# A GFNet filter with a ReGLU gate: the order of all steps written as a list, and the tenth pair of feature tiles multiplied in seven block products

## The chip, the cores and the metric

The kernel runs on one core of a Trainium2 chip. The time is that of the device for one execution, in microseconds (us). Several executions of the kernel before were timed; one more was taken by the hardware profiler, and all rows below are from that one.

The engines are TensorE (PE for matmuls, PEld for the loading of its weights), VectorE (DVE), ScalarE (ACT), GpSimd (POOL) and SyncE (SP), which here starts most DMAs. Each engine works through its own queue of instructions in the order of the program.

## The reference

```python
def _layernorm(x, axis=-1, eps=1e-5):
    m = jnp.mean(x, axis=axis, keepdims=True)
    v = jnp.var(x, axis=axis, keepdims=True)
    return (x - m) / jnp.sqrt(v + eps)
def _A_ref(x, w_r, w_i):                       # the filter
    X = jnp.fft.rfft2(x, axes=(-2, -1)) * (w_r + 1j * w_i)
    return jnp.fft.irfft2(X, s=x.shape[-2:], axes=(-2, -1))
def _B_ref(x, W_gate, W_up, W_down):           # ReGLU
    gate, up = x @ W_gate, x @ W_up
    return (gate * (gate > 0) * up) @ W_down
xn = _layernorm(x)                             # x: 1 x 2048 x 512, fp32
out = x + _A_ref(xn, w_r, w_i) * silu(_B_ref(xn, W_gate, W_up, W_down))
```

W_gate and W_up are 512 x 1376, W_down is 1376 x 512, the filter's weights are 2048 x 257. All is fp32.

## The kernel before

**Precision.** PE multiplies in fp16. Each operand is split into a high part, made by ACT or DVE, and a low part, the rest, made by DVE or POOL (the "lows"). A product is three passes, high x high, high x low and low x high (`PASSES`).

**The filter (branch A).** The two-dimensional transform is done by matmuls with constant matrices. Eight chunks of rows (`NCH`, c = 0 to 7) are loaded (x), normalised (xf), folded by symmetry (`fold`: eo, ee, xs), split (xs16) and multiplied by `first_stage`: a group of 24 matmuls on tiles of 64 (s in the profile), whose result t goes to memory (A_d) and comes back by frequency. Then eight middle chunks (`fft_chunk`) run through the stages y, xx, the multiplication with the weights wt on DVE and POOL (xsp, tt, pf), z and v. Last `last_stage` (again small tiles) and the unfolding by DVE give the filter's rows sv.

**The ReGLU (branch B).** Rows are taken in four blocks of 512 (c = 0 to 3), the 1376 features in eleven tiles of 128, the last one of 96. `turn` splits xf into x16 and transposes it by a DMA of SP's queue into xT, two chunks to a block, so block 1 needs chunks 2 and 3 (x16_2, x16_3). For each tile `product` makes gate and up (gu, 12 matmuls 128x512 each), `rectify` the ReLU of gate (r, on ACT), `hidden` the product h32 (DVE) and its split h16. `down` multiplies h16 with the split W_down (wds) into dn, one step of three matmuls for each tile and row group; `gate` takes silu (g). `down_weights` makes wds from the loaded W_down in place: the high of slot f (ACT) reads slot f + 1, and the low of slot f (DVE) reads it too, so that ACT's next slot waits for DVE's low. In the last block the last row group of dn is made in three pieces of columns: 256, 128 and 128 (`columns`).

**Fast pairs.** `PAIRS` joins ten of the tiles to five pairs. For a pair `fast_products` makes gate and up of both tiles in seven products of 12 matmuls 128x256 (sa, sb, sc), after the scheme of Strassen and Winograd, where the plain way takes four products of 12 matmuls 128x512. It needs the sums of rows xS (`row_sums`) and of weights wT (`weight_sums`), two copies on ACT (sb from sa, sk from sc) and two more adds on DVE (sc, se). Whether a pair is fast in block c is said by `fast(c, n)` from the table `FASTS`: with '2' from block 2 on, with '1' in block 3 alone. Before, pair 1, tiles 3 and 4, has '1', so nine pairs of blocks 2 and 3 are fast.

**The order.** Nothing runs while the kernel's functions are called. Each calls `step` (engine, cost, a function that issues the instructions, what it reads and writes), and `Plan` collects the steps. `Plan.run` then is a list scheduler: from a due time for each step (`DUES`), the leads of loads (`WAITS`), costs and the room of the buffers (`ROOM`) it picks the next step of an engine, with a bonus for PE to stay with tiles of one size. The steps are issued in the order that comes out. Buffers are taken in that order too, so which buffer a tile gets, and whom it waits for, follows from it.

A helper records every instruction, so nearly all rows of the profile have that one line (L200).

```python
def fast(c, n):
    return c >= NBL - int(FASTS[n])
```

Of the kernel before, what the change touches and what calls it, by code (L numbers as in the profile page):

```python
# [1572 lines left out]
```

## Time and profile before

| what | value |
|---|---|
| median of three runs | 400.47 us |
| the runs | 401.05, 399.61, 400.47 us |
| profiled execution: span | 399.6 us |
| PE busy | 391.2 us, 3332 matmuls |
| DVE, ACT, POOL busy | 329.2, 247.2, 72.3 us |
| moved by DMA | 69.55 MB, 174 GB/s on the mean |

The profiled execution lies at the lowest of the timed runs and 0.87 us below their median. In a row of the profile, `out<-in` are the program's names of what is written and read; `xN` is the number of instructions; what stands in brackets is the idle time ahead of a row and what ended it. The chain of waits goes back from the last instruction to what released each step.

Two coarser lines of the page show how the work lies over the span, in 40 slices of 10 us, each digit a busy share in tenths:

```profile
DVE  3899998998888997669986888988769863887995
ACT  6997986868576666845568865535335542754422
```

DVE is nearly full in the first 150 us and again at the end; ACT is fullest in the first 60 us.

### The profile page before, as it was taken

To read this page: it belongs to the slowest core of one execution; us is meant where nothing else is said; L and a number is where in the kernel's file an instruction comes from. 1 tells how busy PE (TensorE), PEld (TensorE's weight loads), DVE (VectorE), ACT (ScalarE), POOL (GpSimd) and SP (SyncE) were. 2 spreads that over 40 slices of the span, in tenths; PEclk is the share of its full clock that TensorE was granted. 3 is DMA by queue.
4 is the path that set the end of the run, shared out by engine and by line. 5 is a ranking of instruction groups with operands and counts; after the bars stand their busy time and mean duration, and the time that the engine had idled before them with its cause. 6 is when DMAs were issued, how large, how long until landed. Compare 5 with 4: busy or idle time off the path is not lost.

```text
span 399.6 us, 8608 instructions
## 1 busy us (share of the span) xinstructions
PE 391.2 (98%) x3332; PEld 243.8 (61%) x3332; DVE 329.2 (82%) x726; ACT 247.2 (62%) x479; POOL 72.3 (18%) x79
## 2 busy tenths in 40 slices
PE   6999999999999999999999999999999999999995
PEld 5965444544445444456585777776567878787544
DVE  3899998998888997669986888988769863887995
ACT  6997986868576666845568865535335542754422
POOL 1004300000000000051405391413212301122211
PEclk9899999999999999999999999999999999999999
DMA  7972311327812998997878790536543048998496
GB/s 272 407 230 63 106 54 34 100 55 178 294 55 51 307 307 244 279 268 167 215 222 246 223 241 22 146 81 199 153 125 107 2 106 183 228 296 167 133 239 158
DMA packets 59353, 69.55 MB, mean 174 GB/s; under 512 B 24688, under 2 KB 36560, under 8 KB 59312
## 3 DMA queue, kind: packets, MB, share of 16 engines
q1 hardware_dynamic: 57872, 66.38, 57.2%
q0 software_dynamic: 1440, 2.62, 4.3%
q8 instruction: 26, 0.43, 0.4%
q14 instruction: 15, 0.12, 0.1%
HBM read 43.81 MB, written 22.56 MB: 166 GB/s over the span
## 4 chain that ended last, share of the span: by engine, by line
PE 82%; DVE 8%; DMA 4%; ACT 3%; issue 2%; SPq 0%; DVEq 0%; ACTq 0%; POOLq 0%
PE dn L200 26%; PE gu L200 26%; PE sb L200 8%; PE sc L200 5%; PE sa L200 5%; PE z L200 3%; PE xx L200 3%; PE s L200 2%; DVE wgu L200 2%; PE y L200 2%; PE v L200 2%; DMA out<-sv 2%; DMA x<-in_x 2%; DVE sv L200 1%; ACT wgu L200 1%
## 5 line engine op out<-in xcount | busy, mean ns | idle before, releaser
L200 PEld LDWEIGHTS <-wgu 128*128 128x128 f16 x960 | 93.0, 98 | 65.3 <-issue 2.9
L200 PE MATMUL dn<-wds,h 128*128 128x512 f16 (+2 forms) x528 | 118.2, 373 | 0.3 <-DVE h L200 0.3
L200 PE MATMUL gu<-xT,wgu 128*128 128x512 f16 (+1 forms) x528 | 112.0, 369 | 0.4 <-DVE xT L200 0.4
L200 PEld LDWEIGHTS <-h 128*128 128x128 f16 (+1 forms) x594 | 53.5, 98 | 54.4 <-issue 2.8
L200 POOL TENSOR_TENSOR rp<-rp,rp 128x512 f32<-128x512 f32 x9 | 12.1, 1354 | 132.9 <-DVE pw L200 125.5
L200 PEld LDWEIGHTS <-wT 128*128 128x128 f16 x324 | 31.2, 98 | 6.1 <-issue 1.0
L200 PE MATMUL sb<-xS,wT 128*128 128x256 f16 x216 | 26.6, 273 | 0.0
L200 PE MATMUL sa<-xT,wgu 128*128 128x256 f16 x216 | 26.5, 273 | 0.0
L200 ACT ACTIVATE r<-gu 128x512 f32<-128x512 f32 (+2 forms) x26 | 14.9, 574 | 16.2 <-PE gu L200 16.2
L200 DVE TENSOR_TENSOR h<-gu,r 128x512 f32<-128x512 f32 (+3 forms) x34 | 20.6, 607 | 5.0 <-ACT h L200 3.5
L200 ACT ACTIVATE h<-h 128x512 f16<-128x512 f32 (+1 forms) x26 | 16.1, 624 | 11.8 <-DVE h L200 11.8
L200 DVE SCALAR_TENSOR_TENSOR tt<-xsp,cw,wt 128x512 f32<-128x512 f32 x32 | 22.8, 755 | 0.1
L200 ACT ACTIVATE g<-dn,cdi 128x512 f32<-128x512 f32 (+1 forms) x16 | 10.8, 673 | 16.5 <-PE dn L200 16.5
L200 DVE TENSOR_TENSOR h<-h,h 128x512 f16<-128x512 f32 (+1 forms) x26 | 18.3, 705 | 1.8 <-ACT h L200 1.7
L200 POOL TENSOR_TENSOR tt<-tt,tt 128x256 f32<-128x256 f32 x10 | 9.5, 957 | 43.1 <-DVE tt L200 41.1
L200 PE MATMUL gu<-xT,wgt 128*64 128x256 f16 (+1 forms) x144 | 17.0, 309 | 0.0
L200 ACT ACTIVATE a<-y 128x1024 f16<-128x1024 f32 x8 | 8.2, 1024 | 12.8 <-PE y L200 6.1
L200 DVE SCALAR_TENSOR_TENSOR wgu<-raw,p,wgu 128x512 f16<-128x512 f32 x20 | 15.1, 772 | 0.0
L200 POOL TENSOR_TENSOR pf<-tt,tt 128x256 f32<-128x256 f32 x12 | 11.3, 947 | 18.9 <-DVE tt L200 16.6
L200 DVE TENSOR_TENSOR a<-y,a 128x1024 f16<-128x1024 f32 x8 | 9.8, 1224 | 5.6 <-ACT a L200 5.5
L200 ACT ACTIVATE rp<-rp,csc 128x512 f32<-128x512 f32 x20 | 13.5, 713 | 1.1 <-DMA rp<-in_wg 1.1
L200 PEld LDWEIGHTS <-wgt 128*64 128x64 f16 (+1 forms) x144 | 9.6, 106 | 6.6 <-issue 1.3
(208 smaller groups left out, 701.2 us busy)
## 6 DMA issues: line engine op xcount, KB each, us to landing
A_d<-t SPq DMA_DIRECT2D x16, 256.0 KB, 3.8
rw<-in_wl SPq DMA_DIRECT2D x8, 512.0 KB, 5.2
wt<-in_wl SPq DMA_DIRECT2D x8, 512.0 KB, 5.5
at<-A_d SPq DMA_DIRECT2D x8, 512.0 KB, 5.1
C_d<-t SPq DMA_DIRECT2D x16, 256.0 KB, 3.5
ct<-C_d SPq DMA_DIRECT2D x16, 256.0 KB, 6.8
x<-in_x SPq DMA_DIRECT2D x7, 512.0 KB, 5.7
G_d<-g SPq DMA_DIRECT2D x12, 256.0 KB, 3.6
```

Of the source, the lines that this page charges most:

```text
L200: return lambda *args, **kw: self.tc.keep_in_program_order(f(*args, **kw))
```

## The change

The scheduler goes, and with it its two tables of numbers, `DUES` and `WAITS`. In their place stands one list, `ORDER`, of 1678 numbers: the steps are issued in this order. In `FASTS` the second entry goes from '1' to '2', so that pair 1 is fast in block 2 as well, and ten pairs are fast. Its sums of weights are thus made ahead of block 2 and no longer ahead of block 3. The number of steps goes from 1671 to 1678: on PE 424 to 427, DVE 553 to 555, ACT 411 to 413; POOL (73) and SP (210) keep theirs.

```diff
-FASTS = ['2', '1', '2', '2', '2']
+FASTS = ['2', '2', '2', '2', '2']
-DUES = (
-    78.44, 124.64, 138.03, 130.55, 999999976, 999999994, 999999984, 999999989, 999999991, 999999984, 999999981, 999999975, 999999987, 999999960,
...
-WAITS = (
-    34.96, 5.86, 10.55, 96.13, 0.66, 8.25, 139.72, 229.23, 74.47, 110.72, 71.7, 201.18, 86.45, 49.12, 48.58, 203.18, 90.2, 18.44, 50.66, 82.96, 4.33,
...
+ORDER = (
+    4, 5, 46, 6, 7, 8, 9, 10, 11, 12, 47, 71, 13, 70, 14, 15, 16, 17, 18, 19, 20, 21, 22, 23, 24, 25, 26, 228, 27, 28, 29, 30, 
...
     def run(self):
-        steps = self.steps
-        for s in reversed(steps):
...
-        for t, s in order:
-            s.fn()
+        for n in ORDER:
+            self.steps[n].fn()
```

The order moves over the whole program: a step stands on the mean 9 places (PE), 13 (DVE), 11 (ACT) or 13 (SP) from where it stood on its engine, some up to 170. Over the whole order PE's visits to groups of small tiles (s, y, z, v and the like, several groups in one visit) go from 31 to 25. The first product of block 1, gu1_0_0, stands right behind the last products of block 0 and one group of s (s1_2); before, all dn of block 0, the groups s1_0 and s1_1 and the product gu1_0_1 stood ahead of it, and 24 matmuls of dn and s1_0 were among the last products of block 0. The last dn of all is the piece of 128 columns, before it was that of 256. At the head of the program PE transposes the first rows (head) ahead of the `small` that sums m0, which it did behind it before, and ACT copies that head to xTf with no row of x2 in front, where xf2 stood in front of it.

Three places show what the rows look like (after a name the number of its buffer's use; L200 is the helper's line before, L154 after). First, DVE at about 60 us of the span: the splits of the rows x16_2, the folding eo1 of chunk 1 and the weights wds. Before:

```order
L200 TENSOR_REDUCE max_md_127<-rows_md_802 128x1
L200 TENSOR_TENSOR h32_0_5_822<-gu0_5_1_690,r0_5_704 128x512
L200 SCALAR_TENSOR_TENSOR wgu6_100<-raw6_1_655,p6_766,wgu6_100 128x512
L200 TENSOR_TENSOR xs16_2_820<-xs2_630,xs16_2_820 128x2x512
L200 TENSOR_TENSOR h32_0_7_841<-gu0_7_1_806,r0_7_789 128x512
L200 TENSOR_TENSOR xs0_711<-eo0_688 128x2x128
L200 TENSOR_SCALAR scd_114<-rho_108,pd_128 128x11
L200 TENSOR_TENSOR h16_0_5_825<-h32_0_5_822,h16_0_5_825 128x512
L200 SCALAR_TENSOR_TENSOR wds_107<-wds_107,scd_114 128x512
```

And now:

```order
L154 TENSOR_TENSOR x16_2_812<-xf2_461,x16_2_812 128x512
L154 TENSOR_REDUCE max_md_127<-rows_md_863 128x1
L154 TENSOR_TENSOR xs0_896<-eo0_835 128x2x128
L154 TENSOR_SCALAR scd_114<-rho_108,pd_128 128x11
L154 TENSOR_TENSOR xs16_2_882<-xs2_791,xs16_2_882 128x2x512
L154 TENSOR_TENSOR eo1_937<-xf1_309 128x2x257
L154 SCALAR_TENSOR_TENSOR wds_107<-wds_107,scd_114 128x512
L154 TENSOR_TENSOR h32_0_7_943<-gu0_7_1_839,r0_7_855 128x512
L154 TENSOR_TENSOR ee0_948<-eo0_835 128x2x129
L154 SCALAR_TENSOR_TENSOR wds_107<-wds_107,scd_114 128x512
```

The lows of x16_2 have moved up ahead of this place, and eo1, which takes the buffer of x16_2, stands between them and the first low of wds. The first of these rows is the second half of x16_2.

SP's queue at the same place holds the transposing DMAs of block 1's rows (xT1). Before they stand behind the stores of t:

```order
L200 DMA x4_796<-in_x 128x1024
L200 DMA x5_905<-in_x 128x1024
L200 DMA A_d_69<-t1_2_898 128x1x1024 x2
L200 DMA out_0<-in_x 128x512
L200 DMA A_d_69<-t1_0_960 128x1x1024 x2
L200 DMA_TRANSPOSE xT1_1122<-x16_2_1016 128x16x128
L200 DMA_TRANSPOSE xT1_1122<-x16_3_1059 128x16x128
```

Now:

```order
L154 DMA x5_724<-in_x 128x1024
L154 DMA_TRANSPOSE xT1_796<-x16_3_750 128x16x128
L154 DMA x4_800<-in_x 128x1024
L154 DMA_TRANSPOSE xT1_796<-x16_2_812 128x16x128
L154 DMA s4_130<-in_sp 128x16
L154 DMA out_0<-in_x 128x512 x2
L154 DMA A_d_69<-t1_2_968 128x1x1024 x2
```

Both transposes have moved up, that of x16_3 ahead of that of x16_2, and the loads of x4 and x5 stand between and before them.

Second, ACT somewhat later, where r0_8 reads the product gu0_8_0, whose buffer gu1_0_0 takes. Before:

```order
L200 ACTIVATE r0_7_789<-gu0_7_0_748 128x512
L200 ACTIVATE wgt_106<-raw6_0_383,p6_766 128x4x96
L200 ACTIVATE wgu6_100<-raw6_0_383,p6_766 128x512
L200 ACTIVATE r0_8_804<-gu0_8_0_776 128x512
L200 ACTIVATE xs16_2_820<-xs2_630 128x2x512
L200 ACTIVATE h16_0_5_825<-h32_0_5_822 128x512
```

Now:

```order
L154 ACTIVATE wds_107<-wds_107,scd_114 128x512 x2
L154 ACTIVATE t1_2_968<-s1_2_909 128x2x448
L154 ACTIVATE h16_0_6_971<-h32_0_6_793 128x512
L154 ACTIVATE wds_107<-wds_107,scd_114 128x512
L154 ACTIVATE t1_2_968<-s1_2_909 128x2x64
L154 ACTIVATE xf4_991,st4_992<-x4_800 128x512
L154 ACTIVATE r0_8_996<-gu0_8_0_865 128x512
```

r0_8 has moved from ahead of the first wds to behind four of them.

Third, DVE in block 2, at the last pair (2,9) of it, whose add sc2_4 stood and stands behind work of the middle chunks (xsp, tt). Before:

```order
L200 TENSOR_TENSOR sr2_3_3221<-sb2_3_3119,sr2_3_3221 128x512
L200 TENSOR_TENSOR p16_3_3399<-pf_3_3358,p16_3_3399 128x1024
L200 TENSOR_TENSOR xsp_4_3415<-xx4_3385,xo4_3418 128x256
L200 SCALAR_TENSOR_TENSOR tt3_4_3454<-xsp_4_3415,cw_110,wt_4_3027 128x512
L200 SCALAR_TENSOR_TENSOR tt2_4_3456<-xsp_4_3415,cw_110,wt_4_3027 128x512
L200 SCALAR_TENSOR_TENSOR tt1_4_3472<-xsp_4_3415,cw_110,wt_4_3027 128x512
L200 TENSOR_TENSOR sc2_4_3420<-sb2_4_3433,sk2_4_3452 128x512
```

Now:

```order
L154 TENSOR_TENSOR sr2_3_3632<-sb2_3_3409,sr2_3_3632 128x512
L154 TENSOR_TENSOR t9_4_3648<-v4_3611,t9_4_3648 128x2x512
L154 TENSOR_TENSOR h16_2_2_1_3577<-se2_2_3307,h16_2_2_1_3577 128x512
L154 TENSOR_TENSOR h16_2_3_0_3653<-sr2_3_3632,h16_2_3_0_3653 128x512
L154 TENSOR_TENSOR xsp_5_3712<-xx5_3655,xo5_3672 128x256
L154 SCALAR_TENSOR_TENSOR tt2_5_3724<-xsp_5_3712,cw_110,wt_5_3359 128x512
L154 SCALAR_TENSOR_TENSOR tt1_5_3726<-xsp_5_3712,cw_110,wt_5_3359 128x512
L154 SCALAR_TENSOR_TENSOR tt3_5_3728<-xsp_5_3712,cw_110,wt_5_3359 128x512
L154 TENSOR_TENSOR sc2_4_3675<-sb2_4_3670,sk2_4_3718 128x512
```

The middle chunk beside the pair is the fifth and no longer the fourth, and between sr2_3 and the add a store's split t9_4 and two h16 have come in where p16_3 stood.

More of the change, by code (lines that the diff above doesn't have):

```diff
@@ L62 @@
 TICK, TICK_TO = 1.16, 60
-FASTS = ['2', '1', '2', '2', '2']
+FASTS = ['2', '2', '2', '2', '2']
 XDUE, SDUE = [-44.18, 1.62, 81.91, 105.7, 173.95, 99.44, 177.4, 146.02], [-114.62, 32.24, 147.09, 211.35]
 DEVIATE = (2.68, 2.54, 2.54)
-DUES = (
-    78.44, 124.64, 138.03, 130.55, 999999976, 999999994, 999999984, 999999989, 999999991, 999999984, 999999981, 999999975, 999999987, 999999960,
-    999999983, 999999975, 999999990, 999999987, 1.00000001e+09, 999999988, 999999984, 999999986, 1e+09, 999999973, 999999995, 999999991, 999999991,
-    999999989, 999999986, 999999992, 999999993, 999999994, 1.00000001e+09, 999999994, 999999964, 999999992, 999999995, 999999996, 999999996,
-    999999999, 999999999, 999999984, 999999993, 1.00000002e+09, 999999998, 999999999, -215.98, -223.3, -206.7, -40.58, -39.53, -42.57, -38.17,
[87 rows of a table removed]
-)
-WAITS = (
[13 rows of a table removed]
+ORDER = (
[62 rows of a table added]
 )
@@ L255, in run @@
     def run(self):
-        steps = self.steps
-        for s in reversed(steps):
-            s.due = 1e9 if s.due is None else s.due
-            for d in s.deps:
-                t = s.due - d.cost - d.lag
-                d.due = t if d.due is None else min(d.due, t)
-        for s, due in zip(steps, DUES):
-            s.due = due
-        for s, lead in zip([s for s in steps if s.lead is not None], WAITS):
-            s.lead = lead
-        for s in steps:
-            if s.due > CALM and s.engine == "SP":
-                s.lag += SAFE_LAG
-            elif s.due > CALM and s.engine != "PE":
-                s.cost *= SAFE
@@ L271, in run @@
-        base = lambda n: n[0] if isinstance(n, tuple) else n
-        users, holds = {}, {}
-        for s in steps:
-            holds[s] = {base(n) for n in [*s.names, s.holder] if base(n) in self.tiles}
-            for n in holds[s]:
-                users[n] = users.get(n, 0) + 1
-        room = {t: [0.] * n for t, n in self.room.items()}
-        live, last = set(), {}
-        free = dict.fromkeys(("PE", "DVE", "ACT", "POOL", "SP"), 0.)
-        ports = {"DVE": 0., "POOL": 0.}
-        dma, todo, order, mode, port = 0., {e: [] for e in free}, [], 0, None
@@ L282, in run @@
-        waiting = {s: len(s.deps) for s in steps}
-        after = {}
-        for s in steps:
-            for d in s.deps:
-                after.setdefault(d, []).append(s)
-            if not s.deps:
-                todo[s.engine].append(s)
-        for _ in steps:
-            best = None
-            for e, mine in todo.items():
-                at = []
-                for s in mine:
-                    t = max([free[e]] + [d.end + (0. if d.engine == e == "PE" else d.lag + s.margin) for d in s.deps])
-                    if s.lead is not None:
-                        t = max(t, s.due - s.lead)
-                    if s.port:
-                        t = max(t, ports["POOL" if e == "DVE" else "DVE"])
-                    need = {}
-                    for n in holds[s] - live:
-                        tag = self.tiles[n][0]
-                        need[tag] = need.get(tag, 0) + 1
-                    if any(len(room[tag]) < k for tag, k in need.items()):
-                        continue
-                    for tag, k in need.items():
-                        t = max(t, sorted(room[tag])[k - 1] + .15)
-                    at.append((t, s))
-                if at:
-                    soon = min(t for t, _ in at) + .06
-                    now = [k for k in at if k[0] <= soon]
-                    if e == "PE" and mode:
-                        now = [k for k in now if 0 < k[1].mode < 3 and k[1].due < k[0] + JOIN] or now
-                    t, s = min(now, key=lambda k: (e == "PE" and k[1].mode != mode if mode else 0, k[1].due, k[1].order))
-                    late = [k for k in at if soon < k[0] <= t + .5 * s.cost and k[1].due < min(s.due, k[0]) + HURRY]
-                    if late and e in ("ACT", "DVE"):
-                        t, s = min(late, key=lambda k: (k[1].due, k[1].order))
-                    turns = best and s.port and best[1].port and {e, best[1].engine} == {"DVE", "POOL"} and abs(t - best[0]) < .03
-                    if best is None or (e != port if turns else t < best[0]):
-                        best = t, s
-            assert best, "no step can begin"
-            t, s = best
-            e = s.engine
-            todo[e].remove(s)
-            for n in holds[s]:
-                if n not in live:
-                    live.add(n)
-                    r = room[self.tiles[n][0]]
-                    r.remove(min(r))
-            if e == "PE":
-                t, mode = t if s.mode == mode else max(t, free[e] + MODE), s.mode
-            free[e] = t + s.cost
-            s.end = free[e]
-            if s.kb:
-                if s.block:
-                    s.end = free[e] = max(s.end, dma + s.block)
-                dma = max(dma, s.end) + s.kb / (340 if t < CALM else RATE)
-                s.end = dma
-            if s.port:
-                ports[e], port = s.end, e
-            for n in holds[s]:
-                users[n] -= 1
-                last[n] = max(last.get(n, 0.), s.end + s.lag)
-                if not users[n]:
-                    room[self.tiles[n][0]].append(last[n])
-            order.append((t, s))
-            for a in after.get(s, ()):
-                waiting[a] -= 1
-                if not waiting[a]:
-                    todo[a.engine].append(a)
@@ L351, in run @@
-        order.sort(key=lambda k: k[0])
-        self.log = order
-        for t, s in order:
-            s.fn()
+        for n in ORDER:
+            self.steps[n].fn()
 def dve(n):
```

161 rows, old and new, of tables (DUES, ORDER, WAITS) are left out of this document.

## The prediction

> **What bounds the kernel now.** I read the page first, then PE's waits, then the chain of waits in order of time, then windows of the start, and last the timelines of DVE and ACT where the change puts something new.
>
> ```profile
> PE 391.2 (98%) x3332; PEld 243.8 (61%) x3332; DVE 329.2 (82%) x726; ACT 247.2 (62%) x479; POOL 72.3 (18%) x79
> PEclk9899999999999999999999999999999999999999
> PE 82%; DVE 8%; DMA 4%; ACT 3%; issue 2%; SPq 0%; DVEq 0%; ACTq 0%; POOLq 0%
> ```
>
> PE is busy for 98% of the span at nearly full clock and holds 82% of the chain; the next engine, DVE, has 82% of the span to do. The waits of PE, all of them, are these (total, times, longest):
>
> ```profile
> PE gu L200 <- ACT xTf L200: 1.4, 1, 1.4
> PE small L200 <- DVE md L200: 1.1, 1, 1.1
> PE small L200 <- ACT wgu L200: 0.6, 1, 0.6
> PE gu L200 <- DVE xT L200: 0.4, 1, 0.4
> PE dn L200 <- DVE h L200: 0.3, 1, 0.3
> ```
>
> The first four lie ahead of 22 us; the last is at 377.8. Between them PE never waits. So the span is start + PE's work + tail, and a change can do four things: alter PE's work, alter the start, alter the tail, or make PE wait where it does not wait now. A written order in place of the scheduler's can do all four. One more thing belongs to the start:
>
> ```profile
> 0.00:60.00 60.00, 56.54 (x337) 36.28 (x338) 49.98 (x157) 50.74 (x126) 9.48 (x19) 0.97 0.55 188
> 7.14:10.55 3.41, 1.60 (x12) 1.32 (x13) 1.98 (x9) 2.32 (x8) 0.00 (x0) 1.00 1.02 401
> 10.55:13.96 3.41, 3.41 (x18) 3.41 (x18) 2.54 (x8) 3.41 (x9) 0.00 (x0) 0.50 1.04 412
> ```
>
> (Columns: length, busy PE, PEld, DVE, ACT, POOL, then the granted clock, DMA share, GB/s.) After a stretch in which PE was busy for 1.60 of 3.41 us, the clock was 0.50 for the next 3.41 us. That costs half of it, 1.7 us of PE's work.
>
> **The change part by part.** The sum is made against the profiled execution, span 399.6, which is 0.87 below the median of the runs, 400.47; I carry differences over to the median.
>
> *1. The start, up to block 1's first product.* To compare like with like I take the moment when PE has done all products of block 0 and one group of s, which is what the new order puts ahead of gu1_0_0. Before, by the chain (start, us):
>
> ```profile
> 67.51 1.94 PE dn L200 x9
> 69.46 0.78 PE s L200 x24
> 70.24 1.40 PE dn L200 x6
> ...
> 74.23 0.65 PE dn L200 x3
> ...
> 77.47 1.29 PE dn L200 x6
> 78.76 1.43 PE gu L200 x24
> ```
>
> The products of block 0 end at 78.76 + 1.43 = 80.19. The four pieces of dn (5.28) and this second group of s (0.78) go behind gu1_0_0 in the new order: 80.19 - 5.28 - 0.78 = 74.13. Two gains may bring PE there sooner. The first is at the head of the program:
>
> ```profile
> 7.80 0.64 PE L200 MATMUL head<-unit,xf 128*128 128x128 f32 x4
> ...
> 9.31 0.58 ACT L200 ACTIVATE xTf<-head 128x512 f32<-128x512 f32 x1
> ```
>
> The head ends at 8.44, but ACT copies it only from 9.31 on, since a load of x2 held xf2 ahead of the copy. In the new order nothing of x2 is ahead: 0.87. And head is no longer behind the `small` that waited 0.6 for wgu; half of that makes it 1.2. The second gain is the half clock (1.7), which a fuller window may spare. So PE arrives between 74.13 and about 71.2 (74.13 - 2.9); I take the middle, 72.6.
>
> PE may not start then, since gu1_0_0's buffer comes free only with ACT's r0_8. r0_8 stands in ACT's queue behind a ladder of wds pairs, where every ACT half waits for the DVE half before it, and the first DVE half stands behind eo1, which takes the buffer that the second transposing DMA reads (x16_2). That DMA comes from about 88 us down to about 60; ahead of it in SP's queue are now the other transpose and two loads of x. Its landing is the unknown:
>
> ```profile
> x<-in_x SPq DMA_DIRECT2D x7, 512.0 KB, 5.7
> x<-in_x SPq DMA_DIRECT2D x2, 256.0 KB, 2.6
> L200 SPq DMA_TRANSPOSE xT<-x x2: 1802/2210/2617, 87.9 to 90.6; - x2
> xS<-S_d SPq DMA_TRANSPOSE x4, 8.6
> ```
>
> The two transposes took 1.8 and 2.6 us on the queue; how long from issue to landing isn't shown. Bounds are 2.6 (a small load, also about the longer of the two queue times) and 8.6 (the other kind of transposing DMA); I take 5.7, the load with the same 512 KB. Then the ladder, by these rows of DVE and ACT:
>
> ```profile
> 61.50 0.69 DVE L200 TENSOR_TENSOR h<-gu,r 128x512 f32<-128x512 f32 x1
> 68.33 0.74 DVE L200 SCALAR_TENSOR_TENSOR wds<-wds,scd 128x512 f16<-128x512 f32 x1
> ...
> 69.11 0.72 ACT L200 ACTIVATE wds<-wds,scd 128x512 f16<-128x512 f32 x1 [0.96 <-DVE wds L200]
> 69.73 0.61 ACT L200 ACTIVATE h<-h 128x512 f16<-128x512 f32 x1
> 71.28 0.90 ACT L200 ACTIVATE t<-s 128x896 f16<-128x896 f32 x1
> ```
>
> Successive rows overlap by some 0.1, which I take off. From T0, the end of the second low of x16_2 on DVE: 5.7 to the landing; eo1 and a wds on DVE, 0.69 + 0.74 - 0.1 = 1.3; four more rows of DVE and the next wds, 1.8 (h 0.6, the rest short); then on ACT wds 0.65, t 0.83, h 0.53, wds 0.63, a short t 0.2, xf and r0_8 0.6 each, 4.0. Together 12.8. T0: by 60.00 DVE had begun 157 instructions, and the low is the 159th of the new order; two more at 60/157 = 0.38 us give 60.8, and I take 61.0. gu1_0_0 starts at 61.0 + 12.8 = 73.8, after a wait of 1.2, against 74.1: **-0.3**. Bounds: with a landing of 2.6 PE's own arrival decides, 71.2, so -2.9; with 8.6 it is 76.7, +2.6.
>
> *2. The tenth pair.* Pair (3,4) of block 2:
>
> ```profile
> 222.41 2.59 PE gu L200 x12
> 225.00 1.31 PE sb L200 x12
> ```
>
> Four plain products (gu) cost 4 x 2.59 = 10.36, seven fast ones (sb) 7 x 1.31 = 9.17: **-1.19**, all of it on PE, which waits for nothing there. The sums of weights are the same work, only earlier. Two copies on ACT and two adds on DVE come in (0.61 and 0.69 each); ACT, idle for 38% of the span, hides its part; DVE's part is in point 4. If the products had to wait for them all the gain would be gone, 2 x (0.61 + 0.69) = 2.6 against 1.19.
>
> *3. Fewer changes between small and large tiles.* The chain shows s groups (small tiles) alone and in one go:
>
> ```profile
> 341.07 0.78 PE s L200 x24
> 341.86 1.42 PE sc L200 x12
> ...
> 345.48 1.31 PE sa L200 x12
> 346.79 1.44 PE s L200 x48
> ```
>
> Two groups in one visit take 1.44, apart 1.56: 0.12 saved. The product behind a visit takes 1.42 instead of 1.31: 0.11 more. A visit saved is worth 0.23, or about 0.11 an edge. In the new order the visits fall from 31 to 25, one of them ahead of gu1_0_0; five at 0.23 give 1.15, less two edges that come in within visits: **-0.95**. The bounds are 0 (the edges hidden behind weight loads) and -1.4 (six whole visits).
>
> *4. New waits in block 2.* Ahead of the add sc2_4 on DVE now stand, from the product sr2_3 on, t9_4, two h16, three parts of xsp and three tt:
>
> ```profile
> 66.19 1.22 DVE L200 TENSOR_TENSOR xs<-xs,xs 128x1024 f16<-128x1024 f32 x1
> ...
> L200 DVE SCALAR_TENSOR_TENSOR tt<-xsp,cw,wt 128x512 f32<-128x512 f32 x32 | 22.8, 755 | 0.1
> ```
>
> t9_4 as the 1024-wide row, 1.22; h16 2 x 0.69; xsp 0.8 (512 columns in three parts); tt 3 x 0.755 = 2.27; the add 0.69; less 0.65 of overlaps: 5.7 us from the time when sr2_3 ends. PE has three fast products and two pieces of dn in that time, 3 x 1.31 + 2 x 0.65 = 5.2: a wait of 0.5. Behind PE's waiting product in its queue is everything else. Two other places of blocks 2 and 3 read alike with less in front, 0.3 each: together **+1.1**, bounds 0 (DVE is early there) and 2.1 (each twice as late).
>
> *5. The end.* The wait of 0.3 for h goes: **-0.3**. The last down piece becomes 128 columns wide, before it was 256:
>
> ```profile
> 395.01 0.47 ACT L200 ACTIVATE g<-dn,cdi 128x256 f32<-128x256 f32 x1 [2.92 <-PE dn L200]
> 395.51 0.42 DVE L200 TENSOR_TENSOR sv<-sv,g 128x256 f32<-128x256 f32 x1 [1.05 <-ACT g L200]
> ...
> 390.75 0.37 ACT L200 ACTIVATE g<-dn_3bb,cdi 128x128 f32<-128x128 f32 x1 [0.32 <-PE dn_3bb L200]
> ...
> 65.99 0.29 DVE L200 TENSOR_TENSOR t<-s,t 128x128 f16<-128x128 f32 x1 [0.97 <-ACT t L200]
> ```
>
> ACT 0.47 - 0.37 = 0.10, and DVE twice 0.42 - 0.29 = 0.13: **-0.36**, plainly behind PE's last matmul.
>
> Sum: -0.3 - 1.19 - 0.95 + 1.1 - 0.3 - 0.36 = -2.0. Span 399.6 - 2.0 = 397.6; time 400.47 - 2.0 = **398.5**.
>
> **The rivals.**
>
> *Slower: the transposing DMA is late.* It lands after 8.6, as xS does; for it speaks that two loads of 512 KB and another transpose are in the queue just ahead, against it that its queue times are no longer than 2.6. gu1_0_0 then starts at 76.7, 2.9 later than forecast: -2.0 + 2.9 = +0.9. PE has waited 76.7 - 72.6 = 4.1 by then, so some stretch of 3.41 has no more than the 1.60 of busy time that brought the half clock above, and 1.7 more are lost: 400.47 + 2.6 = **403.1**. It decides from a landing of about 7 on, where the wait passes 2 us. The Trainium skill, "TensorE: Matmul & The Clock Gate", Part 1: The HAM clock gate, says that the clock halves after an idle window of about 3.4 us that runs freely; by that rule a stretch with 1.60 of work is not idle, so the row above disagrees unless partial work counts, and this rival would end near 401.4 unless the wait covers such a window whole.
>
> *No change: DVE's queue.* DVE has only 18% of its time left and its order is now fixed. If the three waits of point 4 are twice as long (+1.1 more) and the edges of point 3 save half (+0.5), the sum is -0.4 and the time 400.47 - 0.4 = **400.1**. For it: three tt rows in a block ahead of an add; against: before had DVE rows of the same kind in front of the same add without a wait of PE. Here belongs also the case that the tenth fast pair gives nothing since its copies hold PE.
>
> *Better: the start gives more.* Landing by 4 us or less and no half clock: gu1_0_0 at about 72.2, another -1.6: 400.47 - 3.6 = **396.9**.
>
> **How the numbers follow.** Chances: forecast 0.45 (own range 397.6 to 399.8, from points 3 and 4); late DMA 0.15; no change 0.22; better 0.18. A measurement tells 0.3%, 1.2 us, from no change: bounds 399.27 and 401.67. Faster: 0.18 of the better case and 0.39 of the forecast's 0.45, 0.57. Slower: the late DMA and 0.01, 0.16. Same: 0.27. The range runs from 396.6 (a little under the better case) to 401.6 (no change with the worst waits, and the late DMA without the half clock); about 0.15 is left above and 0.05 below.
>
> **What would show it.** Point 1: gu1_0_0 near 73.8 with ACT r as its releaser, and a clock row of 1.00 at 10 to 14 us or again 0.50. Point 2: seven sa, sb, sc groups of 1.31 for pair (3,4) in block 2. Point 3: PE's work behind gu1_0_0 shorter by about 2.1. Point 4: three new rows in PE's waits with DVE sc or sb. Point 5: last matmul to end of span shorter by 0.36. A wait of PE of over 2 us anywhere, or a half clock past 22 us, would make the forecast wrong.

## The result and the profile after

| | before | after |
|---|---|---|
| median of six runs each, on one chip | 400.13 us | 402.80 us |
| lowest and highest | 399.20 to 401.05 us | 401.52 to 404.79 us |
| ratio after to before, 95% interval | | 1.0065 (1.0038 to 1.0092) |
| span of the profiled execution | 399.6 us | 401.7 us (its time 403.46) |

The change made the kernel 0.65% slower, 2.7 us; forecast were 2.0 us less. The time of a run is 1.8 us more than its span (403.46 to 401.7, and so in every run). The six runs after are of two kinds: with a mean granted clock of 0.999 they took 401.52, 401.71 and 402.14 us, with 0.992 to 0.994 403.46, 403.70 and 404.79. A stretch of 3.41 us at half clock takes 0.0042 off the mean; the profiled run, of the second kind, has one in the middle of the program. Against the 400.13 of before, the first kind is some 1.6 us slower (its median is 401.71) and the second some 3.6 (403.70). One execution of number 8 below took 506.68 us at a mean granted clock of 0.755 and is in none of the comparisons.

Busy time, the granted clock in 40 slices, and the chain by engine, from the page after:

```profile
PE 389.3 (97%) x3368; PEld 248.4 (62%) x3368; DVE 337.7 (84%) x728; ACT 244.9 (61%) x481; POOL 73.3 (18%) x79
PEclk9999999999999999999999999899999999999999
PE 46%; DVE 15%; DMA 2%; ACT 1%; issue 1%; ACTq 0%; DVEq 0%
```

PE has 1.9 us less to do, DVE 8.5 us more, of which the two new adds are 1.4. The shares of the chain add up to only 65%, since it is followed back no further than 135 us; in that part DVE holds 15%, where it held 8% of the whole chain before. The lower clock has moved from the second slice (10 us) to the 26th (250 us). PE's waits after, those of 0.7 us or more:

```profile
PE gu L154 <- DVE t L154: 2.2, 1, 2.2
PE sc L154 <- DVE sr L154: 2.0, 1, 2.0
PE small L154 <- ACT wgu L154: 1.1, 1, 1.1
PE small L154 <- DVE md L154: 1.1, 1, 1.1
PE gu L154 <- ACT r L154: 0.9, 2, 0.5
PE z L154 <- ACT xsp L154: 0.7, 1, 0.7
```

Three are new and lie in the middle of the program: 2.2, 2.0 and 0.7 us. Before, nothing behind 22 us waited longer than 0.3. Where they stand, with the first product of block 1 ahead of them, in PE's timeline (start, length; in brackets the idle time in front and who ended it):

```profile
72.53 2.75 PE L154 MATMUL gu<-xT,wgu 128*128 128x512 f16 x12 [0.47 <-ACT r L154]
...
148.32 4.20 PE L154 MATMUL gu<-xT,wgt 128*64 128x256 f16 x36 [2.20 <-DVE t L154]
...
200.46 1.50 PE L154 MATMUL z<-cD,p 128*128 128x128 f16 x24 [0.71 <-ACT xsp L154]
...
252.80 2.43 PE L154 MATMUL sc<-xS,wgu 128*128 128x256 f16 x12 [1.99 <-DVE sr L154]
```

gu1_0_0 starts at 72.53. The last row is one fast product, which takes 1.31 elsewhere; here it takes 2.43. Windows of the start, of the 3.41 us around that wait and of the 3.41 us that follow (columns as before):

```profile
10.24:13.65 3.41, 3.41 (x33) 3.41 (x33) 3.11 (x13) 3.41 (x10) 0.00 (x0) 1.00 1.04 419
249.72:253.13 3.41, 1.42 (x19) 0.68 (x17) 3.03 (x4) 0.89 (x1) 2.20 (x2) 1.00 0.00 0
253.13:256.54 3.41, 3.41 (x59) 2.50 (x56) 3.21 (x4) 2.80 (x6) 0.00 (x0) 0.50 0.00 0
```

The half clock at the start is gone; another one begins at 253.13, right behind the wait of 2.0. So each profile has one such stretch, and they cancel between the two. The difference of the spans, +2.1, adds up: up to gu1_0_0 -1.6 (72.53 against 74.13, with the half clock of before in it); the three new waits +4.9, the old one of 0.3 gone; the half clock at 253.13 +1.7 (half of 3.41); the tail behind PE's last matmul, 3.9 against 4.6, -0.7; and as the remainder PE's work behind gu1_0_0, -1.9. The same terms nearly give the medians. Most runs of before have no half clock (number 7), and against these the start is worth -1.6 + 1.7 = +0.1. The sum is then an estimated +2.1 for the first kind of run and +3.8 for the second; measured were the 1.6 and 3.6 above.

**Why DVE is late.** DVE and POOL in the stretch ahead of the first new wait, which is for the row t at 147.19:

```profile
143.23 1.19 DVE L154 TENSOR_SCALAR h<-s 128x16 f32<-128x16 f32 x1
144.46 1.33 DVE L154 TENSOR_TENSOR spw<-h 128x8 f32<-128x8 f32 x2
145.71 0.25 DVE L154 TENSOR_TENSOR edge<-edge 128x16 f32<-128x16 f32 x2
145.91 1.23 DVE L154 TENSOR_SCALAR edge<-edge 128x16 f32<-128x16 f32 x1
147.05 0.22 DVE L154 TENSOR_SCALAR edge<-edge,cS 128x16 f32<-128x16 f32 x1
147.19 1.08 DVE L154 TENSOR_TENSOR t<-s,t 128x896 f16<-128x896 f32 x1
...
143.12 1.28 POOL L154 TENSOR_TENSOR rp<-rp,rp 128x512 f32<-128x512 f32 x1 [90.42 <-DVE t L154]
144.47 1.29 POOL L154 TENSOR_TENSOR rp<-rp 128x512 f32<-128x512 f32 x1
145.84 2.60 POOL L154 TENSOR_TENSOR rp<-rp,rp 128x512 f32<-128x512 f32 x2
```

And the same small rows of DVE before, where POOL had nothing to do at that time:

```profile
130.28 0.17 DVE L200 TENSOR_SCALAR h<-s 128x16 f32<-128x16 f32 x1
130.49 0.24 DVE L200 TENSOR_TENSOR spw<-h 128x8 f32<-128x8 f32 x2
...
134.09 0.17 DVE L200 TENSOR_SCALAR edge<-edge 128x16 f32<-128x16 f32 x1
```

A row of 16 columns takes 1.19 where it took 0.17. Each long row ends just when a row of POOL does (144.42 and 144.40; 145.79 and 145.76; 147.14, about half through the pair that starts at 145.84): DVE's row is held until POOL's is done, some 1.05 us for each. Three of them make t 3.2 late. The row t<-s,t itself, which reads PSUM (the memory of PE's results), runs beside POOL in 1.08, as it does elsewhere (1.09 in run 1 below). POOL's rows are the sums of weights (rp) for a fast pair; the written order has put them beside these rows. Held rows as such are not new: before, two rows wgu<-rp at 236 us took 2.58 beside POOL's sums, where one takes 0.42 without them, but no wait of PE came of it.

The same stands ahead of the second wait, for the row sr at 252.07:

```profile
246.31 1.75 DVE L154 TENSOR_TENSOR wT<-rp,wT 128x512 f16<-128x512 f32 x1
247.99 1.21 DVE L154 TENSOR_TENSOR z<-z,z 128x1024 f16<-128x1024 f32 x1
249.12 3.03 DVE L154 TENSOR_TENSOR pf<-tt 128x128 f32<-128x128 f32 x4
252.07 0.68 DVE L154 TENSOR_TENSOR sr<-sb,sr 128x512 f32<-128x512 f32 x1
...
249.26 2.74 POOL L154 TENSOR_TENSOR rp<-rp,rp 128x512 f32<-128x512 f32 x2
```

Here wT, and two of the four small rows pf, are held. Between the two places lies the wait of 0.7, at 200 us. PE's z waits for ACT's xsp there, and that for DVE, whose small rows at 190 to 196 us stand beside POOL's sums for pair 1:

```profile
189.96 3.15 DVE L154 SCALAR_TENSOR_TENSOR zt<-zd,cw,spw 128x4 f32<-128x4 f32 x4
...
194.59 1.97 DVE L154 TENSOR_TENSOR pf<-tt 128x128 f32<-128x128 f32 x4
...
199.81 0.60 ACT L154 ACTIVATE xsp<-xx 128x512 f32<-128x512 f32 x1 [1.20 <-DVE xsp L154]
```

Before, the same four rows zt took 0.62 and the four pf 0.89. Nor has DVE time to catch up between the places; windows before, then after:

```profile
210.00:250.00 40.00, 40.00 (x424) 28.94 (x420) 31.76 (x44) 30.16 (x49) 19.54 (x16) 1.00 0.65 181
...
210.00:250.00 40.00, 40.00 (x436) 30.33 (x433) 38.44 (x61) 25.07 (x41) 12.59 (x12) 1.00 0.59 170
```

DVE (third number) is busy for 38.44 of 40 us after, 31.76 before. A full DVE alone is not enough for a wait, though: in number 10 below it is busy for 38.38 us of the same 40, none of its rows there is beside a sum of POOL, and PE waits for nothing behind 172 us.

### The profile page after: what moved, and what is told of

Same layout as the page of the kernel before. It is cut to its first block, busy times and chain, and to the rows that moved or that the text cites. A ratio compares the mean times of both kernels' runs of the same rounds, so it can differ in the third digit from the quotient of the medians.

```text
span 401.7 us, 8677 instructions
## 1 busy us (share of the span) xinstructions
PE 389.3 (97%) x3368; PEld 248.4 (62%) x3368; DVE 337.7 (84%) x728; ACT 244.9 (61%) x481; POOL 73.3 (18%) x79
## 4 chain that ended last, share of the span: by engine, by line
PE 46%; DVE 15%; DMA 2%; ACT 1%; issue 1%; ACTq 0%; DVEq 0%
PE dn L154 13%; PE sb L154 9%; PE sc L154 6%; PE sa L154 5%; PE gu L154 5%; DVE tt L154 3%; DMA X_d<-x 2%; DVE pf L154 2%; PE z L154 2%; PE xx L154 2%; PE s L154 1%; PE v L154 1%; PE y L154 1%; DVE h L154 1%; DVE t L154 1%
## 5 line engine op out<-in xcount | busy, mean ns | idle before, releaser
L154 PEld LDWEIGHTS <-wgu 128*128 128x128 f16 x960 | 93.7, 99 | 63.7 <-issue 6.1
L154 PE MATMUL dn<-wds,h 128*128 128x512 f16 (+2 forms) x528 | 117.9, 372 | 0.0
L154 PE MATMUL gu<-xT,wgu 128*128 128x512 f16 (+1 forms) x480 | 101.7, 368 | 1.0 <-ACT r L154 0.9
L154 PEld LDWEIGHTS <-h 128*128 128x128 f16 (+1 forms) x594 | 54.7, 98 | 52.8 <-issue 0.6
L154 PEld LDWEIGHTS <-wT 128*128 128x128 f16 x360 | 34.8, 98 | 6.7 <-issue 0.9
L154 PE MATMUL sb<-xS,wT 128*128 128x256 f16 x240 | 29.5, 273 | 0.1
L154 PE MATMUL sa<-xT,wgu 128*128 128x256 f16 x240 | 29.5, 273 | 0.0
L154 POOL TENSOR_TENSOR rp<-rp,rp 128x512 f32<-128x512 f32 x9 | 11.7, 1304 | 90.9 <-DVE t L154 90.4
L154 ACT ACTIVATE g<-dn,cdi 128x512 f32<-128x512 f32 (+1 forms) x16 | 10.4, 671 | 25.4 <-PE dn L154 22.3
L154 DVE SCALAR_TENSOR_TENSOR tt<-xsp,cw,wt 128x512 f32<-128x512 f32 x32 | 22.4, 746 | 1.1 <-ACT xsp L154 0.7
L154 DVE TENSOR_TENSOR h<-gu,r 128x512 f32<-128x512 f32 (+3 forms) x32 | 19.3, 602 | 2.9 <-PE gu L154 1.7
L154 PE MATMUL gu<-xT,wgt 128*64 128x256 f16 (+1 forms) x144 | 17.0, 309 | 2.2 <-DVE t L154 2.2
L154 ACT ACTIVATE p<-pf 128x1024 f16<-128x1024 f32 x8 | 8.4, 1054 | 16.9 <-DVE pf L154 16.9
L154 ACT ACTIVATE h<-h 128x512 f16<-128x512 f32 (+1 forms) x24 | 14.8, 620 | 5.0 <-DVE h L154 4.9
L154 POOL TENSOR_TENSOR pf<-tt,tt 128x256 f32<-128x256 f32 x12 | 9.1, 778 | 47.3 <-DMA S_d<-sx 31.9
L154 PE MATMUL sc<-xS,wgu 128*128 128x256 f16 x120 | 15.7, 284 | 2.0 <-DVE sr L154 2.0
L154 POOL TENSOR_TENSOR tt<-tt,tt 128x256 f32<-128x256 f32 x10 | 10.8, 1089 | 30.2 <-DVE tt L154 30.2
L154 DVE TENSOR_TENSOR h<-h,h 128x512 f16<-128x512 f32 (+1 forms) x24 | 16.3, 684 | 0.0
L154 ACT ACTIVATE a<-y 128x1024 f16<-128x1024 f32 x8 | 8.2, 1023 | 12.0 <-PE y L154 11.8
L154 ACT ACTIVATE r<-gu 128x512 f32<-128x512 f32 (+2 forms) x24 | 13.3, 569 | 3.3 <-PE gu L154 3.2
L154 DVE TENSOR_TENSOR sc<-sb,sk 128x512 f32<-128x512 f32 x10 | 7.0, 696 | 9.8 <-PE sb L154 6.6
L154 DVE SCALAR_TENSOR_TENSOR wgu<-raw,p,wgu 128x512 f16<-128x512 f32 x20 | 14.6, 745 | 0.6 <-ACT wgu L154 0.5
```

Of the source, the lines that this page charges most:

```text
L154: return lambda *args, **kw: self.tc.keep_in_program_order(f(*args, **kw))
```

## The experiments

All start from the changed kernel unless another start is named; ORDER is edited as a list of steps. Medians stand beside the kernel before, run in the same batch.

**1. POOL's sums of pair 0 behind the small rows.**

```diff
-461, 683, ..., 787, 792, 376, 535, 1649, 532, 534, 793, ..., 437, 520
+461, 683, ..., 376, 535, 1649, 532, 534, ..., 437, 787, 792, 793, 802, 803, 794, 800, 795, 798, ..., 520
```

> The changed kernel with one thing moved: the weight sums of the first pair (the last scaling of rp0 on ACT, POOL's four subtractions on rp0 and the steps that read them) are issued some 10 us later; DVE's rows between 142 and 148 us keep their order. Theory A (DVE instructions are held by POOL instructions beside them): in the changed kernel the rows h<-s, spw<-h and edge<-edge at 143 to 147 us took 1.19, 1.24 and 1.23 us beside POOL's rp, in the kernel before 0.16 to 0.17; without POOL they are at 0.2 or less again, the t behind them ends some 3 us sooner, PE's wait of 2.2 us (gu from DVE t) falls under 0.3, and the time is 2.0 us below the changed kernel's. Theory B (DVE's queue is simply too long there): the rows keep their lengths, the wait stays over 1 us and the time moves by less than 0.5 us.

Measured: 403.78 against 400.13, ratio 1.0092 (1.0075 to 1.0108). DVE's rows are short again, and the wait of 2.2 is gone:

```profile
143.05 0.17 DVE L154 TENSOR_SCALAR h<-s 128x16 f32<-128x16 f32 x1
...
143.62 0.17 DVE L154 TENSOR_SCALAR edge<-edge 128x16 f32<-128x16 f32 x1
```

So POOL's rows hold them. But the time got no better: `PE dn <- DVE h` now waits 2.8 us at 162, since the readers of the sums have moved too and wait for POOL: DVE stands idle for 2.97 us ahead of wgu.

**2. The row sr ahead of pf.**

```diff
-1352, 1353, 872, 935, 1354
+1352, 935, 1353, 872, 1354
```

> The changed kernel with one DVE step moved by one place: the product sr2_2 (it frees the buffer that PE's sc2_3 takes) stands ahead of the four pf rows and no longer behind them. Theory A: two of these pf rows took 1.36 and 1.35 us beside POOL's rp, and PE's wait of 2.0 us at 250.8 (sc from DVE sr) is that; with sr ahead the wait goes, and with it the half clock of the 3.41 us behind it (1.7 us): 2.0 us below the changed kernel in runs where it had kept its clock, 3.7 us where it had not, and no run under a granted clock of 0.998. Theory C (the clock halves there for another reason): the wait goes, a half clock at about 250 us stays in some runs, 2.0 us.

Measured: 403.21 against 400.13, ratio 1.008 (1.0065 to 1.0096). The wait of 2.0 is gone. Two of 1.0 stand in its place (z for DVE's t, sb for ACT's copy), and the half clock stands at 147, behind the wait of 2.2.

**3. Both edits.**

> Both moves of the two runs before in one kernel. Theory A: the waits of 2.2 and 2.0 us and the half clock go, 4.2 us below the changed kernel in runs with full clock, 5.9 in the others; about 398 us, some 2 us below the kernel before. Theory D (what is taken from PE's waits is given back at the next one, since DVE's work as a whole sets the time): less than 2 us below the changed kernel, and new waits of PE for DVE elsewhere.

Measured: 404.13 against 400.13, ratio 1.0106 (1.0087 to 1.0125). Both large waits are gone, and 2.8, 1.0 and 1.0 are there, with the half clock behind the 2.8. Moving single rows moves the waits.

**4. The new order with nine pairs.** Pair 1 is plain again in block 2, and its sums are made some 320 steps later.

```diff
-FASTS = ['2', '2', '2', '2', '2']
+FASTS = ['2', '1', '2', '2', '2']
```

> The changed kernel's order with nine pairs: pair (3,4) of block 2 by four plain products at the places of its seven fast ones, and its weight sums about 320 steps later, ahead of block 3. If the tenth pair is worth 1.19 us of PE's work and nothing else: 1.2 us above the changed kernel. If its weight sums cost by collision (POOL's rp1 beside DVE's zt rows at 190 to 196 us, where four rows took 1.0 to 1.1 us more than alone, and PE's wait of 0.7 us at 199.8 behind them): the rows at 190 to 196 us are short again, that wait is gone, and the time is only 0.5 us above, or less.

Measured: 403.63 against 400.13, ratio 1.0094 (1.0073 to 1.0116). Three of its four runs have full clock, at 403.2 to 403.8 us; the changed kernel at full clock took 401.5 to 402.1. Between the medians of these (403.49 and 401.71) the tenth pair is worth 1.8 us even with its waits (forecast 1.19). Without it the waits at 200 and 251 vanish, but beside the 2.2, which stays, others come:

```profile
PE z L154 <- ACT a L154: 1.2, 1, 1.2
...
PE z L154 <- DVE t L154: 1.0, 1, 1.0
...
PE z L154 <- ACT g L154: 0.6, 1, 0.6
```

The loss lies in the order, not in the pair.

**5. The small rows of 143 us ahead of POOL's sums.** The steps 535 (h, spw) and 532 (edge) go up, so nothing has to wait for POOL.

```diff
-414, 401, 417, 461, ..., 376, 535, 1649, 532, 534
+414, 535, 532, 401, 417, 461, ..., 376, 1649, 534
```

> The changed kernel with the two DVE steps of small rows (h<-s, spw<-h and edge<-edge) issued some 3 us sooner, ahead of the low of x16_6, so that they run before POOL begins with rp; everything else keeps its order and POOL its place. Theory A (held rows): the rows take 0.2 us or less, the t behind them ends about 3 us sooner, PE's wait of 2.2 us at 146 goes, and no other takes its place, since now nothing is moved that others wait for: 2.2 us below the changed kernel. Theory D (DVE has no room from 165 to 252 us, so PE is held there instead): the wait at 146 goes, but PE's waits for DVE between 160 and 260 us grow by about as much, from 2.7 us to 4.5 or more, and the time moves by less than 0.8 us, apart from the half clock.

Measured: 401.13 against 400.49, ratio 1.0026 (1.0009 to 1.0044). The wait of 2.2 is gone, and only 3 of 10 runs had a half clock (402.3 to 403.1). The waits of 0.9 (z) and 2.0 (sc) stay, and 1.0 (xx for max_mw, at 171) comes in. Between runs at full clock the gain is 0.8 us (medians 400.89 and 401.71): far less than theory A's 2.2, and about theory D's bound. From the restart of z to that of sc it is 52.35 us, as in the changed kernel (52.34), though z restarts 0.7 us sooner: that fits a stretch in which DVE sets the pace.

**6. Number 5, and sr and a copy of ACT (944) earlier.**

```diff
-1352, 1353, 872, 935, 1354, 944, 1355
+1352, 935, 1353, 872, 944, 1354, 1355
```

> The run before, with sr2_2 ahead of the pf rows on DVE and ACT's copy sb2_3 ahead of the high of p16_4, which held it for 1.0 us in the run with sr first. Theory A: the waits of 2.2 and 2.0 us are gone, of the two waits of 1.0 us only the z for t is left; 3.2 us below the changed kernel in dip-free runs and 4.9 in the others: about 398. Theory D: PE waits for DVE or ACT at other places of 160 to 290 us for 3 us or more, and the time is over 400.5.

Measured: 401.65 against 400.49, ratio 1.0038 (1.0019 to 1.0058). A wait of 2.1 of z for DVE's t takes the place of the 2.0 of sc, and xx waits 1.7 for max_mw; in the profile the half clock stands behind the 2.1 again.

**7. The old order, with only its head changed.** Nine pairs in the order that the scheduler gave before; PE's head ahead of the `small`, xf2 behind xTf.

> The kernel before, in its own order, with two steps moved at the head as the change does: PE's transposing products of the first rows stand ahead of the small that sums m0, and ACT copies head to xTf ahead of the first xf2. If the start was the gain that the forecast took it for: PE's wait of 1.4 us for xTf falls to 0.4 or less, the half clock at 10 to 14 us goes, and PE is 1.0 to 2.6 us sooner at the end of block 0's products. If DVE sets the time from there on, this comes back as waits of PE for DVE before 165 us and the time moves by less than 0.5 us; otherwise the kernel is 1.0 to 2.6 us faster than before.

Measured: 400.01 against 400.49, ratio 0.9991 (0.998 to 1.0003). No half clock at the start, no wait over 1.1, span 398.2, but in the median at most half a microsecond. Most runs of before can't have had that half clock either: of 87 beside these experiments, 62 have a mean granted clock of 0.998 or more, while 3.41 us at half clock in 399.6 take 0.0043 off it. Only five of the 87 had a span of 399.6 or more. The run also shows that a written list costs nothing by itself.

**8. Number 5, with low parts of sx16_3 (440 to 442) some places later.** It asks whether these 1024-wide rows make the wait at 171, and DVE's lateness behind it.

```diff
-529, 440, 727, ..., 728, 441, 530, ..., 745, 442, 808, ..., 1253, 730, ..., 1258, 1260
+529, 727, ..., 728, 530, ..., 745, 808, ..., 1253, 440, 730, ..., 1258, 441, 442, 1260
```

> The run with the corners first, and besides the split of the row sums sx16_3_1 (ACT, DVE and its store) issued some 25 steps later. In that run ACT's sx waits until the store X_d of chunk 7, whose buffer it takes, has landed at about 170 us; behind it in ACT's queue stand the copies of y0, behind its low in DVE's queue max_mw, and DVE is idle for up to 2.9 us. Theory E (what the corners gave was lost again at that one place): PE's wait of 1.0 us at 171 (xx from max_mw) goes, the z at 199 waits 0.3 or less and the sc at 250 0.8 or less, no half clock there; about 2.5 us below the run with corners first, at 398.5. Theory D (DVE has too much to do between 171 and 252 us, whoever starts sooner): the wait at 171 goes, those at 199 and 250 stay within 0.5 us of 0.9 and 2.0 in sum, and the time falls by less than 1 us.

Measured: 401.50 against 400.65, ratio 1.0027 (1.001 to 1.0044). The wait at 171 is gone, 1.1 (dn) has come at 179, and 0.9 (z) and 2.0 (sc) stand as before, 52.36 us apart. So those two don't come from what is late at 171.

**9. Numbers 6 and 8, and PE's groups z4 (1356) and v4 (1359) some places later.**

```diff
-950, 1356, 1369, 948, 951, 952, ..., 955, 1359, 876, ..., 964, 1360
+950, 1369, 948, 951, 1356, 952, ..., 955, 876, ..., 964, 1359, 1360
```

> The run with three moves, with sx16_3_1 later as in the run beside it, and on PE the group z4 behind the products sa2_3 and sb2_3 (two products, 2.6 us) and v4 behind sa2_4. Theory E: with DVE sooner and PE's 2.6 us of other work in place of the wait of 2.1 us for t, no wait of PE over 0.5 us is left between 100 and 380 us; 4 us below the run with three moves, about 397.5, some 2.5 us below the kernel before. Theory D: DVE is as late as before and PE waits for it at the next sc or z, 2 us or more between 171 and 300 us; the time is 400 or more.

Measured: 405.79 against 400.65, ratio 1.0123 (1.0103 to 1.0144). A wait of 3.1 at 255, for DVE's sc. Worse; once more the wait is moved and not removed.

**10. Number 5, and the sums of pairs 1 and 4 from POOL to DVE.** Eight more rows of 512 columns on DVE, eight fewer on POOL; sr stands ahead of one of them (872).

```diff
-['POOL', 'POOL', 'DVE', 'DVE', 'POOL']
+['POOL', 'DVE', 'DVE', 'DVE', 'DVE']
...
-1353, 872, 935, 1354
+1353, 935, 872, 1354
```

> The run with the corners first, and besides the eight subtractions of weight sums of pairs 1 and 4 (rp on POOL, 512 columns each) made by DVE at the same places of the order, some 0.7 us each, with sr2_2 ahead of those of pair 4. Theory A+D (DVE sets the time from 185 to 252 us, and POOL's rp costs it more by holding its rows than the work itself): in the run with the corners first DVE's rows lost 3.6 us beside the rp of pair 1 (189 to 195 us: zt, zt, tt, pf) and 3.2 us beside that of pair 4 (245 to 251: wT, pf, pf). DVE now takes 5.5 us of work and loses none of these 6.8: it is 0.8 us sooner at 199, where the z waits 0.2 or less, and 3 us sooner with sr at 250, so that the sc waits 0.5 or less and no half clock follows; the time falls by 1 us or more in spite of the busier engine. Rival F (DVE's load as such decides; held rows are slack): the 5.5 us come on top, PE waits 2 us or more longer for DVE between 185 and 270 us, and the kernel is 2 us or more slower than the run with the corners first.

Measured: **397.97 against 400.22**, ratio 0.994 (0.9921 to 0.996). Both waits, of z and of sc, are gone, and 11 of 12 runs were under 399. From its page, and DVE at the same place as above:

```profile
PE 387.8 (98%) x3368; PEld 247.1 (62%) x3368; DVE 332.7 (84%) x736; ACT 244.9 (62%) x481; POOL 63.4 (16%) x71
...
243.73 0.68 DVE L154 TENSOR_TENSOR wT<-rp,wT 128x512 f16<-128x512 f32 x1
244.33 1.21 DVE L154 TENSOR_TENSOR z<-z,z 128x1024 f16<-128x1024 f32 x1
245.46 0.88 DVE L154 TENSOR_TENSOR pf<-tt 128x128 f32<-128x128 f32 x4
246.27 0.68 DVE L154 TENSOR_TENSOR sr<-sb,sr 128x512 f32<-128x512 f32 x1
246.87 0.68 DVE L154 TENSOR_TENSOR rp<-rp,rp 128x512 f32<-128x512 f32 x1
```

DVE makes eight rows more (736, after 728) and is busy for 5.0 us less, 2.5 of it against number 5 (335.2). wT takes 0.68 for 1.75, the four pf 0.88 for 3.03, and a sum costs 0.68 where it took POOL 1.3.

**11. Number 10, and max_mw (530, 531) ahead of a low of sx16_3.**

```diff
-728, 441, 530, 1217, 776, 531, 805
+728, 530, 531, 441, 1217, 776, 805
```

> The run with the sums on DVE, and besides DVE's max_mw and the scales cw behind it issued ahead of the low of sx16_3_1, which waits until about 170 us for a store to land and holds them. PE's wait of 0.9 us at 170 (xx from max_mw) is the last one behind 72 us. If DVE now has room: the wait goes and the time falls by 0.9 us, to about 397.1. If DVE is still the bound behind it: the wait goes, PE waits 0.5 us or more for DVE between 175 and 260 us, and the time stays within 0.4 us.

Measured: **397.11 against 400.12**, ratio 0.9919 (0.9904 to 0.9934), the best of all and faster than both kernels. PE's three longest waits:

```profile
PE small L154 <- DVE md L154: 1.1, 1, 1.1
PE gu L154 <- ACT r L154: 0.9, 2, 0.5
PE gu L154 <- ACT xTf L154: 0.3, 1, 0.3
```

All lie in the first 73 us; from there to 388.7 us PE is idle for 0.2 us in sum.

**12. The sums on DVE alone, as in number 10, with the small rows left at 143 us.**

> The changed kernel with only the eight subtractions of pairs 1 and 4 made by DVE and sr2_2 ahead of those of pair 4; the corners stay where they were, beside POOL's rp of pair 0. If held rows cost what they cost there and DVE sets the time: the wait of 2.2 us at 146 stays, but is mostly made good by 199 us, since DVE is what is late there and it is now 3.6 us less late; the z waits 0.3 or less, the sc at 250 0.5 or less; a half clock only behind the 2.2; the time is 1 us above that of the run with both, at 399.0, and 3 us or more below the changed kernel. If the corners mattered on their own for the whole 2.2: 400.2.

Measured: 399.40 against 400.12, ratio 0.9986 (0.9974 to 0.9998). The waits of z and sc are gone, the 2.2 at 146 stays. Runs with full clock took 398.6 to 399.2, those with a half clock 399.6 to 400.9. The stretch with the wait and the one behind it:

```profile
145.00:148.40 3.40, 1.20 (x31) 0.98 (x32) 3.40 (x7) 1.64 (x3) 3.08 (x3) 1.00 0.46 154
149.00:152.40 3.40, 3.40 (x18) 1.57 (x14) 3.00 (x6) 2.85 (x7) 0.00 (x0) 0.51 0.86 214
```

So the sums of pairs 1 and 4 on POOL cost the changed kernel 3.4 us (402.80 less 399.40; 2.7 between runs at full clock, 401.71 less 399.06), and the place of the small rows another 1.4 (399.40 less 397.97, number 10; 1.1 at full clock).

## Why the prediction was wrong

It gave 398.5 us, 396.6 to 401.6, with 0.57 for faster; the time was 402.8. The step that failed is the fourth, the new waits.

**Step 4, the new waits: +4.9 where +1.1 was forecast, bounds 0 to 2.1.** The one wait that the prediction worked out, behind the add sc2_4, did not come: no row of PE's waits after names an add sc of DVE. A wait did come one pair sooner, where sc2_3 takes the buffer that sr2_2 frees, but for another reason. The prediction counted the rows of DVE ahead of an add and priced each by its length in the trace of before ("t9_4 as the 1024-wide row, 1.22; h16 2 x 0.69"). It didn't ask what would run on POOL beside them. In the new order POOL's sums stand beside rows of DVE, and a row of 128x16 that is held costs as much as a wide one. Runs 1 and 5 show it for the wait of 2.2, by moving either side away; runs 10 and 12 for the waits of z and sc, by taking the sums off POOL. The prediction had two adds, some 1.4 us, as all that DVE has more to do; it was 8.5. The largest wait was at a place that the prediction hadn't looked at: a product of block 1 behind rows of the filter that take 0.17 to 0.25 in the trace of before.

The Trainium skill has a rule that bears on this and that the prediction didn't use: "SBUF — State Buffer", section "Who interferes with whom", says that GpSimd's only ports are VectorE's second pair, that this pair is an exclusive lock, and that a VectorE instruction with two inputs in SBUF (the memory on the chip that holds the tiles), or in a two-port mode, contends with a GpSimd instruction that reads SBUF, so that the later one is blocked for the whole of the first. The trace agrees: spw and wT, with two such inputs, were held by 1.08 and 1.07 beside rows of POOL of 1.29 and 1.45 us, and t, which reads PSUM, was not held. The rows h and edge, with one input, were held too, by 1.02 and 1.06; whether they ran in a two-port mode isn't shown.

**A half clock behind a wait: +1.7 where 0 was forecast.** The prediction had this mechanism, but in the rival of the late DMA and at 76 us. The DMA wasn't late (gu1_0_0 waited 0.47). The last sentence on what would make the forecast wrong, a wait of over 2 us anywhere or a half clock past 22 us, names what came. It falls in half of the six runs and makes the two kinds.

The traces show why it comes in one place and not in another. In all fourteen profiles the changes of the granted clock lie a whole number of windows of 3.413 us apart, whatever PE does: after, from the end of the half clock at 256.54 to the next drop, at 399.90 behind PE's last matmul, it is 143.36 us, 42 such windows. The wait from 250.81 to 252.80 lay within one window; PE was busy for 1.42 us of it, and the next window had half the clock. In run 1 a longer wait, of 2.84, was cut by an edge at 163.51; its two windows had PE busy for 2.28 and 1.71, and no half clock came, while the wait of 1.98 later in the same execution lay within one window (1.44 busy) and brought it. Of all such windows in the profiles here, from some 7 us on and up to PE's last products, those with 1.48 us of work or less were followed by half clock, those with 1.65 or more were not; of the two between, 1.60 (before) was and 1.59 (run 3) was not. By the Trainium skill, "TensorE: Matmul & The Clock Gate", Part 1: The HAM clock gate, the lower clock comes after an idle window of about 3.4 us, running freely. The traces agree with the free running; they don't with idle, since PE did 1.42 us of work in the window.

**Step 1, the start: -1.6 where -0.3 was forecast** (bounds -2.9 and +2.6), in the profiles, because the half clock of before didn't recur. Most runs of before don't have it either (number 7), so that gain is luck of the execution that was profiled. For the medians it is worth little: run 7 gained 0.5 at most.

**The base.** The prediction set the span, 399.6, against the median time, 400.47, and took the profiled execution for a quick one. With the 1.8 us around the span it took some 401.4, and only five of 87 runs of before were as slow. Carried over rightly, -2.0 would have given 399.4 rather than 398.5 for that execution, still far from the result.

**Steps 2 and 3, the tenth pair and the visits: -1.9 where -2.1 was forecast.** The -1.9 is the remainder of the sum. Run 4 gives 1.8 for the pair with its waits, more than the 1.19 forecast, and leaves next to nothing for the visits; but they weren't measured by themselves.

**Step 5, the end: -1.0 where -0.66 was forecast** (the old wait of 0.3 gone, the tail -0.7).

**The rival "DVE's queue"** had the right engine and too small a price: 400.1, with waits twice as long as forecast. They were more than four times as long. What it missed is the held rows, and that DVE, at 38.44 of 40 us, doesn't make up what it loses by them. In runs 1, 2, 3, 6, 8 and 9 a wait that was removed came back in another place.

Not settled: the tenth pair in the old order alone wasn't tried. Where the windows lay in the runs without a profile isn't seen, so that they explain the two kinds of run is argued from the profiles.

## What to carry to other kernels

Price a row in a written order by what runs beside it on the other engines, not by its length in the old trace: beside a GpSimd row a tiny VectorE row can cost that row's whole length. Where an engine is full, moving rows only moves the wait; make its work shorter, here by taking eight sums from GpSimd onto the full VectorE itself. Compare a profiled execution with a run's time only after adding what lies around its span.

## What the runs showed of the hardware

- A VectorE row of 8 or 16 columns was held by a GpSimd row of 1.3 us as long as one of 512 columns, 1.02 to 1.08 us each. Eight more rows on VectorE made it 2.5 us less busy (337.7 to 335.2 in number 12, where nothing else changed but the place of sr). With the eight rows themselves, 0.68 each, that is 7.9 us of held time gone: on GpSimd each sum cost VectorE about 1 us, on VectorE it costs 0.68.
- It goes the other way too. POOL after, the same row at two times:

```profile
184.94 3.50 POOL L154 TENSOR_TENSOR tt<-tt,tt 128x256 f32<-128x256 f32 x1 [2.95 <-DVE tt L154]
...
189.79 0.71 POOL L154 TENSOR_TENSOR tt<-tt,tt 128x256 f32<-128x256 f32 x1
```

The first stands beside VectorE rows without a gap between them (h, two tt, p, to 187.86) and ends 0.58 after the last of them, about its own length. That fits a row held until then; no run tests it.
- One wait of PE of 2.0 to 2.8 us was enough for 3.41 us of half clock when it lay within one of the windows, and not when an edge cut it (2.84 in number 1). The half clock costs 1.7 us of PE's work; between the medians of runs with and without it lay 2.0 us in the changed kernel, 2.0 in number 5 and 1.1 in number 12.
